# Attention's scores and values in 64x64 quarters of TensorE, and output stores into disjoint views, in an attention and two-MoE kernel

## The chip, the cores and the metric

The kernel runs on one core of one Trainium2 chip. The metric is the device time in microseconds (us) of one execution, as the median of several. Engines are named as the profile does: PE is TensorE, PEld its weight loads, DVE is VectorE, ACT is ScalarE, POOL is GpSimd, SP is SyncE.

## The reference, cut to what matters

Attention runs in chunks of 64 positions, each for itself, and two feed-forward stages follow.

```python
# q, k, v: [8 batches, 8 heads, 576 positions, 64]; chunks of 64 positions
scores = scale * np.matmul(q_c, k_c.transpose(0, 1, 2, 4, 3))
scores = scores - np.max(scores, axis=-1, keepdims=True)
attn = np.exp(scores)
attn = attn / (np.sum(attn, axis=-1, keepdims=True) + 1e-09)
out = np.matmul(attn, v_c)
...
x = out.transpose(0, 2, 1, 3).reshape(4608, 512)
h = x @ w_in
x = (h / (1.0 + np.exp(-h))) @ w_out
...
# each of the 4608 tokens goes to one of 8 experts, by x @ w_gate + bias
out[mask] = gate_w[mask, None] * (np.maximum(x[mask] @ w1[e], 0.0) @ w2[e])
```

Everything is f32. The large matmuls keep their precision by splitting each operand into a high part (type fp32r) and a low part, and by summing three products.

## The kernel before, in words

The 4608 tokens are 36 row tiles of 128 tokens, two chunks of 64 each, and 18 blocks of two tiles. For a tile, all 8 heads are handled at once; a head pair `hp` has the heads 2hp and 2hp+1.

The work has three stages. First, a list drawn up by a small planner (`order_of`, with costs and ranks written by hand) orders the attention of the tiles 0 to 5, the first layer of blocks 0 and 1, and the conversion of the first weights. Its scores (`early`, L478) and values (L521) already use 64x64 quarters of TensorE: 64 rows of the contraction by 64 output columns.

Second, for blocks j = 2 to 17, a loop of 18 steps a block does the first MoE layer of block j: `g1` (L615, 12 matmuls a step) and `g2` (L674 to L676). Between them stand pieces of the attention of the block after, at steps fixed in the lists `EVEN` and `ODD`, so that tile 6 and later tiles take this way. [...] For a tile the pieces are:

- `load_qk` (L357) and `load_nat` for v bring q and k in 32x32 pieces and v by rows, on SyncE's queue.
- `att_Tq` (L376) transposes q on VectorE in 32x32 pieces. `att_Tk` (L383) does so for k, a chunk at a time, and writes into `diag["k"]`, [128, 8 heads, 128], in which chunk c fills the rows and columns of half c; the rest stays zero. `diag_open` (L355) cleared it once on GpSimd.
- `att_S` (L395) has 8 matmuls, one a head: 128 contraction rows, 64 output partitions, 128 columns. The zeros keep the two chunks apart. All scores go to one bank of PSUM. Then follow maximum (L402), subtraction (L406) and exponential (L407).
- `att_norm` divides by the sum.
- `att_PT32` transposes p on TensorE (L434), and ScalarE copies it in two halves into `diag["p"]` (L437).
- `att_PV32` (L443) has 8 matmuls of the same shape, into one bank, and then `xh` (L451, ScalarE) and `xl` (L453, VectorE), the two parts of the MoE layer's input.

Scores, transposed p and values, and the ranks of the router (`place`, L773) share a pool of four banks (`ps_att`). The values of one tile and the scores of the next stand in the same step and so back to back on TensorE. VectorE also does the dot products of the router in these steps.

Third, the second MoE layer works through pairs of slots of 128 tokens each, with the expert's weights: `gather_id`, `gather` (L1086, rows by an indirect DMA on GpSimd's queue), `trans_x` (L1108, transposes the gathered rows on TensorE), `G1` (L1119), `G2` (L1145 to L1147). `finish(u)` scales the pair's two accumulators on ScalarE (L1226) and stores each by an indirect DMA (L1227), on GpSimd's queue too:

```python
for t, a in enumerate(oacc.pop(u)):
    ...
    nc.gpsimd.indirect_dma_start(out=out, out_offset=..., in_=o, ...)
```

Rows beyond a slot's count are dropped by the bounds check. The framework orders accesses to one DRAM tensor: a write to `out` waits until the write before it has landed. A slot for 32 tokens comes last (`lone_h`, `lone_T`, `lone_2`); its value matmuls (L1209) use four strips of 32 columns, and its output is stored at L1216.

Of the kernel before, what the change touches and what calls it, by code (L numbers as in the profile page):

```python
# [8 lines left out]

F32 = mybir.dt.float32  # L10
# [5 lines left out]
ALU = mybir.AluOpType  # L16
AX = mybir.AxisListType
# [3 lines left out]
P = 128  # L21
CH = 64
# [4 lines left out]
LQ = 4  # L27
# [177 lines left out]
def attention_moe_moe_kernel(  # L205
# [14 lines left out]
    nc = tc.nc  # L220
    B, H, S, D = q.shape
# [6 lines left out]
    HP = H // 2  # L228
# [35 lines left out]
    def ps_att():  # L264
        return ps.tile([P, 512], F32, tag="att", bufs=4, name="psa")

    def ps_h():
        return ps.tile([P, 512], F32, tag="h", bufs=2, name="psh")

    def ps_acc():  # L270
        return ps.tile([P, 512], F32, tag="acc", bufs=2, name="psc")

    def t2(name, dt=F32, shape=None):
        return sb.tile(shape or [P, 512], dt, tag="t2", bufs=11, name=name)
# [56 lines left out]
    nat, pairs = {}, {}  # L331
# [14 lines left out]

    late_p, diag = [], {}  # L350

    def diag_open():
        for n in ("k", "p"):
            diag[n] = late_p[0].tile([P, 8, P], F32, name="d" + n)
            nc.gpsimd.memset(diag[n], 0.0)  # L355

    def load_qk(t):  # L357
        x = t4("qk", shape=[P, 2, H, 2, 32])
# [12 lines left out]
    qkT = {}  # L371
# [6 lines left out]

    def att_Tk(t):
        x = nat.pop(("qk", t))  # L380
        for c in range(2):
            rows = slice(c * CH, (c + 1) * CH)
            nc.vector.transpose(  # L383
                diag["k"][rows, :, c * CH:(c + 1) * CH], x[rows, 1].rearrange("p h a d -> p h (a d)")
            )
            yield

    pexp = {}

    def att_S(t):  # L390
        sc = ps_att()
        qt = qkT.pop(("q", t))
        for h in range(H):
            hp, r = divmod(h, 2)
            nc.tensor.matmul(  # L395
                sc[r * CH:(r + 1) * CH, hp * P:(hp + 1) * P], lhsT=qt[:, h * CH:(h + 1) * CH],
                rhs=diag["k"][:, h, :], start=True, stop=True,
            )
        yield
        s3 = sc.rearrange("p (g c) -> p g c", c=CH)  # L400
        mx = sb.tile([P, 8, 1], F32, tag="mx", bufs=2, name="mx")
        nc.vector.tensor_reduce(out=mx, in_=s3, axis=AX.X, op=ALU.max)  # L402
        yield
        p = t2("p")
        p3 = p.rearrange("p (g c) -> p g c", c=CH)
        nc.vector.tensor_tensor(out=p3, in0=s3, in1=mx.to_broadcast([P, 8, CH]), op=ALU.subtract)  # L406
        nc.scalar.activation(out=p, in_=p, func=ACTF.Exp, scale=scale)  # L407
        pexp[t] = p

# [13 lines left out]
    def xT_of(t):  # L423
        j = t // 2
        if j not in xT:
            xT[j] = (t4("xh", F32R, [P, KD, 256]), t4("xl", F32R, [P, KD, 256]))
        return xT[j]

    def att_PT32(t):
        p = pexp.pop(t)  # L430
        pt = ps_att()
        for hp in range(HP):
            cols = slice(hp * P, (hp + 1) * P)
            nc.tensor.transpose(pt[:, cols], p[:, cols], ident)  # L434
        for c in range(2):
            rows = slice(c * CH, (c + 1) * CH)
            nc.scalar.copy(diag["p"][rows, :, c * CH:(c + 1) * CH], pt[rows].rearrange("p (h q) -> p h q", q=CH))  # L437

    def att_PV32(t):
        o, x = ps_att(), nat.pop(("v", t))  # L440
        for h in range(H):
            hp, r = divmod(h, 2)
            nc.tensor.matmul(  # L443
                o[r * CH:(r + 1) * CH, hp * P:(hp + 1) * P], lhsT=x[:, h, :], rhs=diag["p"][:, h, :],
                start=True, stop=True,
            )
        yield
        hi, lo = xT_of(t)
        cols = slice((t % 2) * P, (t % 2 + 1) * P)
        o3 = o.rearrange("p (k t) -> p k t", t=P)  # L450
        nc.scalar.copy(hi[:, :, cols], o3)  # L451
        yield
        nc.vector.tensor_tensor(out=lo[:, :, cols], in0=o3, in1=hi[:, :, cols].bitcast(F32), op=ALU.subtract)  # L453


    held = {}
# [84 lines left out]
    def load_w64(n):  # L541
        if n >= NF:
            return
        which, i = DS[n]
        if which == 0:
            a = conv.tile([P, KD, 2 * P, 2], U32, tag="raw", bufs=RAWB, name="ra")
            nc.sync.dma_start(out=a.rearrange("p k f w -> p k (f w)"), in_=w_in64[i])
        else:
            a = conv.tile([P, 2, 512, 2], U32, tag="raw", bufs=RAWB, name="rb")
            nc.sync.dma_start(out=a.rearrange("p a d w -> p a (d w)"), in_=w_out64[i])  # L550
        raw64[n] = a.rearrange("p a f w -> p (a f) w")
# [511 lines left out]
    oid = {}  # L1063
# [136 lines left out]
    def lone_2(ht):  # L1200

        a = ps_acc()
        n = DM // LQ
        for f in range(FE // P):
            g, i = divmod(f, FE // P // LQ)
            c = slice(i * P + g * LTOK, i * P + (g + 1) * LTOK)
            w = lone_w2[f]
            for m in range(LQ):
                nc.tensor.matmul(  # L1209
                    a[m * LTOK:(m + 1) * LTOK, :n], lhsT=ht[:, c], rhs=w[:, m * n:(m + 1) * n],  # L1210
                    start=f == 0, stop=f == FE // P - 1,
                )
        s = 2 * LONE
        o = t2("o")
        nc.scalar.activation(out=o[:, :n], in_=a[:, :n], func=ACTF.Copy, scale=idg[:, s, 1:2])
        nc.gpsimd.indirect_dma_start(  # L1216
            out=out.rearrange("n (h d) -> (n h) d", h=LQ),
            out_offset=bass.IndirectOffsetOnAxis(ap=oid["out"], axis=0), in_=o[:, :n], in_offset=None,
            bounds_check=LQ * NT - 1, oob_is_err=False,
        )  # L1220

    def finish(u):
        for t, a in enumerate(oacc.pop(u)):
            s = 2 * u + t
            o = t2("o")
            nc.scalar.activation(out=o, in_=a, func=ACTF.Copy, scale=idg[:, s, 1:2])  # L1226
            nc.gpsimd.indirect_dma_start(  # L1227
                out=out, out_offset=bass.IndirectOffsetOnAxis(ap=oid.pop(s), axis=0), in_=o, in_offset=None,
                bounds_check=NT - 1, oob_is_err=False,
            )  # L1230


    with tc.manual_schedule():
# [8 lines left out]
        def heat(n, pw=None):  # L1242

            pw = ps_h() if pw is None else pw
            for _ in range(n):
                nc.tensor.matmul(pw[:, :P], lhsT=ones, rhs=ones, start=True, stop=True)
# [55 lines left out]
        for n, idle in todo:  # L1302
            what = n[0]
            hps = None
            if what == "g1":
                st = n[2] + n[1] * SKEW
                begun = True
                if st not in gps:
                    gps[st] = ps_h()
                hps = gps[st][:, n[1] * 256:(n[1] + 1) * 256]  # L1310
            if idle > 0.3 and (hps is not None or not begun):
                heat(min(40, int(12 * idle)), hps)
            if what in ("qk", "v"):
                load_nat(n[1], what)
            elif what == "D":
                load_w64(n[1])
            elif what in RANK:
                early(*n)
            elif what == "g1":
                g1_mm(n[1], n[2], hps)  # L1320
            elif what == "g2":
                finish_step(n[1], n[2] + LAG)
            elif what in ("th", "g", "gh", "gl"):
                g_pair(*n)
            else:
                convert(*n)
            if n == ("lo", NF - 1):
                conv_cm.__exit__(None, None, None)
                late_cm = tc.tile_pool(name="late", bufs=1)
                late = late_cm.__enter__()  # L1330
                late_p.append(late)
                diag_open()
                wgb = late.tile([P, E, DM], F32, name="wgb")
                nc.sync.dma_start(
                    out=wgb.rearrange("p e d -> p (e d)"),
                    in_=wgt_d.rearrange("(o e) d -> o (e d)", o=1).to_broadcast([P, E * DM]),
                )
                wg.append(wgb)
            elif n == ("g2", 0, 1):
                router_loads()  # L1340
            elif n == ("g2", 0, 6):
                router_gate()
            elif n == ("g2", 0, NF - 4):
                zeros()
            elif n == ("g2", 1, NF - 3):
                router_bias()
            elif n == ("g1", 0, NF - 1):
                load_qk(2 * BLK32)
                load_nat(2 * BLK32, "v")
# [8 lines left out]
        for j in range(2, NB):  # L1358
            last = j == NB - 1
            side = {i: sides.pop(2 * nsteps * (j - 2) + i) for i in range(2 * nsteps)}  # L1360
            if last:
# [7 lines left out]
                for n in range(8):  # L1369
                    i, h = divmod(n, 2)  # L1370
# [99 lines left out]
        for u in range(STEADY):  # L1470
            for d in range(NS):
                if d < 2:
                    s = 2 * u + 2 + d
# [16 lines left out]
        u, d = behind.pop()  # L1490
# [67 lines left out]
```

## Time and profile before

| | |
|---|---|
| median of 3 runs | 1389.08 us (1388.49 to 1391.3) |
| the profiled execution | 1389.06 us |
| its span, first to last instruction | 1387.2 us |
| TensorE busy | 1360.8 us, 98% |
| weight loads | 1218.3 us, 88% |
| VectorE busy | 956.1 us, 69% |
| ScalarE busy | 597.7 us, 43% |
| GpSimd busy | 158.6 us, 11% |
| mean granted clock of TensorE | 0.994 |

Busy time is the time in which at least one instruction of an engine runs. Matmuls overlap in TensorE's pipeline, so an instruction's own duration is longer than its share of the time; the distance of two starts tells what one costs. In the rows below, `x16` counts records, and an f32 matmul leaves two of them, an fp32r matmul or a transpose one. Times in rows are us from the span's start; a mean or a minimum, median and maximum are ns; what stands behind `<-` in brackets is what ended the idle time ahead of an instruction.

### The profile page before, as it was taken

What the parts mean: (1) busy time and instruction counts of PE and PEld (TensorE: products, weight loads), DVE (VectorE), ACT (ScalarE), POOL (GpSimd) and SP (SyncE); (2) the same over time, 40 slices, a digit from 0 to 9 for tenths busy, and PEclk for the clock granted to TensorE, in tenths of its full rate; (3) what the DMA queues carried; (4) which work ended last, traced back from release to release, by engine and by line L of the source; (5) the groups of instructions that cost most, each with busy time, mean ns of one, the idle gap of its engine ahead of it and who ended that gap; (6) DMA issues with size and microseconds to landing.
All of it is one profiled execution on the core that took longest, in us unless ns stands there. A gap on an engine that the chain in (4) does not pass through costs nothing. (4 is left out here: it accounts for less than half of the span.)

```text
span 1387.2 us, 26517 instructions
## 1 busy us (share of the span) xinstructions
PE 1360.8 (98%) x9797; PEld 1218.3 (88%) x9797; DVE 956.1 (69%) x2358; ACT 597.7 (43%) x1220; POOL 158.6 (11%) x177
## 2 busy tenths in 40 slices
PE   8899999999999999999999999999999999999996
PEld 8788888988888888888898898888889889889985
DVE  5987886776777667677677677675577666666661
ACT  5554333333333333333333333342455555555551
POOL 1000000000000000000000000022322323232211
PEclk9899999999999999999999999999999999999999
DMA  9555521221231131132132120141676766667663
GB/s 213 170 166 168 108 50 27 50 55 35 34 61 33 32 62 35 28 62 47 16 62 50 27 48 24 37 117 32 233 261 217 233 214 225 215 222 226 227 194 125
DMA packets 242361, 153.93 MB, mean 111 GB/s; under 512 B 189408, under 2 KB 189446, under 8 KB 242096
## 3 DMA queue, kind: packets, MB, share of 16 engines
q1 hardware_dynamic: 234016, 133.07, 35.9%
q0 software_dynamic: 8208, 19.09, 3.8%
q8 instruction: 79, 1.29, 0.4%
q14 instruction: 58, 0.48, 0.1%
HBM read 132.48 MB, written 19.81 MB: 110 GB/s over the span
## 5 line engine op out<-in xcount | busy, mean ns | idle before, releaser
L615 PE MATMUL psh<-xh,big 128*128 128x256 f32 x2304 | 455.3, 283 | 0.0
L615 PEld LDWEIGHTS psh<-xh,big 128*128 128x128 f32 x2304 | 372.3, 189 | 12.4 <-issue 2.7
L615 PE MATMUL psh<-xl,big 128*128 128x256 f32 x1152 | 324.8, 282 | 0.1
L615 PEld LDWEIGHTS psh<-xl,big 128*128 128x128 f32 x1152 | 217.8, 189 | 9.2 <-DVE xl L532 0.3
L1119 PE MATMUL psh<-xgh,big 128*128 128x256 f32 x1152 | 216.4, 281 | 0.2 <-DVE big L922 0.2
L674 PE MATMUL psc<-big,g 128*128 128x512 f32 x512 | 206.4, 403 | 0.0
L624 DVE SCALAR_TENSOR_TENSOR g<-g,psh 128x256 f32<-128x256 f32 x256 | 107.3, 419 | 143.5 <-ACT g L623 139.9
L675 PE MATMUL psc<-big,g 128*128 128x512 f32 x512 | 202.8, 396 | 0.0
L676 PE MATMUL psc<-big,g 128*128 128x512 f32 x512 | 201.9, 394 | 0.7 <-DVE g L661 0.7
L696 DVE CUSTOM_DVE_ANT_0 dump<-x2t,wgb 128x512 bf16<-128x512 f32 x272 | 185.2, 681 | 8.3 <-ACT x2t L685 6.3
L623 ACT ACTIVATE g<-psh 128x256 f32<-128x256 f32 x256 | 98.0, 383 | 210.1 <-PE psh L615 199.0
L1119 PEld LDWEIGHTS psh<-xgh,big 128*128 128x128 f32 x1152 | 181.5, 188 | 3.7 <-DVE big L922 0.6
L659 ACT CAST g<-g 128x256 fp32r<-128x256 f32 x256 | 104.0, 406 | 153.5 <-DVE g L624 148.2
L1119 PE MATMUL psh<-xgl,big 128*128 128x256 f32 x576 | 161.8, 281 | 0.2 <-DVE xgl L1110 0.2
L1129 DVE SCALAR_TENSOR_TENSOR h<-psh,h 128x256 fp32r<-128x256 f32 x144 | 60.9, 424 | 128.6 <-ACT h L1128 118.1
L1128 ACT ACTIVATE h<-psh 128x256 fp32r<-128x256 f32 x144 | 55.4, 385 | 188.8 <-PE psh L1119 165.2
L793 POOL DMA_INDIRECT perm<-rpg,rdi x36 | 36.4, 1012 | 765.5 <-DVE rdi L792 639.0
L661 DVE TENSOR_TENSOR g<-g 128x256 fp32r<-128x256 f32 x256 | 107.7, 421 | 18.1 <-ACT g L659 18.1
L676 PEld LDWEIGHTS psc<-big,g 128*128 128x128 f32 x512 | 96.1, 188 | 24.4 <-DVE g L661 1.1
L1119 PEld LDWEIGHTS psh<-xgl,big 128*128 128x128 f32 x576 | 108.5, 188 | 3.5 <-DVE xgl L1110 0.5
L674 PEld LDWEIGHTS psc<-big,g 128*128 128x128 f32 x512 | 96.2, 188 | 15.4 <-ACT xh L451 2.4
L675 PEld LDWEIGHTS psc<-big,g 128*128 128x128 f32 x512 | 96.4, 188 | 12.5
(256 smaller groups left out, 2000.1 us busy)
## 6 DMA issues: line engine op xcount, KB each, us to landing
rb<-in_moe_w_dram SPq DMA_DIRECT2D x136, 256.0 KB
wr<-in_moe_w_dram SPq DMA_DIRECT2D x67, 512.0 KB
x2d<-x2t SPq DMA_DIRECT2D x36, 256.0 KB
ra<-in_moe_w_in_dram SPq DMA_DIRECT2D x8, 1024.0 KB
rb<-in_moe_w_out_dram SPq DMA_DIRECT2D x8, 1024.0 KB
qk<-in_q_dram SPq DMA_DIRECT2D x240, 32.0 KB
qk<-in_k_dram SPq DMA_DIRECT2D x240, 32.0 KB
vn<-in_v_dram SPq DMA_DIRECT2D x28, 256.0 KB
```

The source lines that it names most:

```text
L615: nc.tensor.matmul(hps[:, :256], lhsT=w, rhs=x[:, kk, :], start=n == 0, stop=n == 3 * KD - 1)
L623: nc.scalar.activation(out=g, in_=hps[:, :256], func=ACTF.Tanh, scale=0.5)
L624: nc.vector.scalar_tensor_tensor(out=g, in0=g, scalar=1.0, in1=hps[:, :256], op0=ALU.add, op1=ALU.mult)
L659: nc.scalar.copy(gh, g)
L661: nc.vector.tensor_tensor(out=gl, in0=g, in1=gh.bitcast(F32), op=ALU.subtract)
L674: nc.tensor.matmul(a, lhsT=gh[:, c], rhs=wh, start=f == 0, stop=False)
L675: nc.tensor.matmul(a, lhsT=gh[:, c], rhs=wl, start=False, stop=False)
L676: nc.tensor.matmul(a, lhsT=gl[:, c], rhs=wh, start=False, stop=f == NF - 1)
L696: nc.vector.tensor_tensor_reduce(out=dump, in0=x2[j][t], in1=wg[0][:, e, :], scale=1.0, scalar=0.0, op0=ALU.mult, op1=ALU.add, accum_out=l ...
L1119: nc.tensor.matmul(hp[:, :256], lhsT=w[:, part, :], rhs=x[:, :, kk * P:(kk + 1) * P], start=i == 0, stop=i == 3 * KD - 1,)
L1128: nc.scalar.activation(out=gh, in_=hp[:, :256], func=ACTF.Relu)
L1129: nc.vector.scalar_tensor_tensor(out=gl, in0=hp[:, :256], scalar=0.0, in1=gh.bitcast(F32), op0=ALU.max, op1=ALU.subtract)
```

## The change

Scores and values of tile 6 and later are computed without zero blocks. Each head and chunk has a matmul of its own, 64 contraction rows (the chunk's half c) by 64 output partitions (half r, the head's place in its pair) by 64 columns, so there are 16 of them instead of 8, in the order of `quarters()`: c = 0 with r = 0 and 1, then c = 1 with r = 0 and 1, for each head pair. Chunk 0 writes to one bank and chunk 1 to another, so scores take two banks and values two. k and p are transposed into plain tiles (`kT` and `pT`, two buffers each), by one instruction instead of two. Maximum, subtraction, `xh` and `xl` now have one instruction a bank. The zero blocks and their clearing are gone. The stores of the second MoE layer write into three views of `out` that the framework takes as disjoint: the pair's first tile, its second tile, and the last slot.

```diff
-    def diag_open():
-        for n in ("k", "p"):
-            diag[n] = late_p[0].tile([P, 8, P], F32, name="d" + n)
-            nc.gpsimd.memset(diag[n], 0.0)
+    def late_t(name):
+        return late_p[0].tile([P, 512], F32, tag=name, bufs=2, name=name)
...
     def att_Tk(t):
         x = nat.pop(("qk", t))
+        y = qkT["k", t] = late_t("kT")
+        nc.vector.transpose(y, x[:, 1].rearrange("p h a d -> p (h a d)"))
...
+    def quarters():
+
+        for hp in range(HP):
+            for c in range(2):
+                for r in range(2):
+                    yield hp, c, r, slice(c * CH, (c + 1) * CH), slice(r * CH, (r + 1) * CH)
+
+    def att_S(t):
+        sc = ps_att(), ps_att()
+        qt, kt = qkT.pop(("q", t)), qkT.pop(("k", t))
+        for hp, c, r, rows, out_rows in quarters():
+            h = slice((2 * hp + r) * CH, (2 * hp + r + 1) * CH)
+            nc.tensor.matmul(
+                sc[c][out_rows, hp * CH:(hp + 1) * CH], lhsT=qt[rows, h], rhs=kt[rows, h], start=True, stop=True
+            )
+        yield
+        s3 = [x[:, :HP * CH].rearrange("p (g k) -> p g k", k=CH) for x in sc]
+        mx = sb.tile([P, 8, 1], F32, tag="mx", bufs=2, name="mx")
         for c in range(2):
+            nc.vector.tensor_reduce(out=mx[:, c * HP:(c + 1) * HP], in_=s3[c], axis=AX.X, op=ALU.max)
+        yield
+        p = t2("p")
+        p4 = p.rearrange("p (g c k) -> p g c k", c=2, k=CH)
+        for c in range(2):
+            nc.vector.tensor_tensor(
+                out=p4[:, :, c, :], in0=s3[c], in1=mx[:, c * HP:(c + 1) * HP].to_broadcast([P, HP, CH]),
+                op=ALU.subtract,
             )
...
     def att_PT32(t):
...
-        for c in range(2):
-            rows = slice(c * CH, (c + 1) * CH)
-            nc.scalar.copy(diag["p"][rows, :, c * CH:(c + 1) * CH], pt[rows].rearrange("p (h q) -> p h q", q=CH))
+        pT[t] = late_t("pT")
+        nc.scalar.copy(pT[t], pt)
 
     def att_PV32(t):
-        o, x = ps_att(), nat.pop(("v", t))
-        for h in range(H):
-            hp, r = divmod(h, 2)
+        o, x, y = (ps_att(), ps_att()), nat.pop(("v", t)), pT.pop(t)
+        for hp, c, r, rows, out_rows in quarters():
+            h = 2 * hp + r
             nc.tensor.matmul(
-                o[r * CH:(r + 1) * CH, hp * P:(hp + 1) * P], lhsT=x[:, h, :], rhs=diag["p"][:, h, :],
+                o[c][out_rows, hp * CH:(hp + 1) * CH], lhsT=x[rows, h, :], rhs=y[rows, h * CH:(h + 1) * CH],
                 start=True, stop=True,
             )
...
+        for c in range(2):
+            nc.scalar.copy(hi[:, :, cols[c]], o3[c])
+        yield
+        for c in range(2):
+            nc.vector.tensor_tensor(
+                out=lo[:, :, cols[c]], in0=o3[c], in1=hi[:, :, cols[c]].bitcast(F32), op=ALU.subtract
+            )
...
-            out=out.rearrange("n (h d) -> (n h) d", h=LQ),
+            out=outs[2].rearrange("n (h d) -> (n h) d", h=LQ),
...
+    outs = dram_disjoint_views(out, 3)
...
-                out=out, out_offset=bass.IndirectOffsetOnAxis(ap=oid.pop(s), axis=0), in_=o, in_offset=None,
+                out=outs[t], out_offset=bass.IndirectOffsetOnAxis(ap=oid.pop(s), axis=0), in_=o, in_offset=None,
```

## Rows read from the trace of the kernel before

**Rows 1.** Busy: TensorE, weight loads, VectorE, ScalarE, GpSimd; granted clock; DMA share, GB/s
```profile
138.00:891.00 753.00, 752.99 (x5462) 673.04 (x5461) 541.58 (x1556) 275.99 (x645) 30.33 (x30) 1.00 0.23 44
891.00:1374.00 483.00, 478.33 (x3116) 430.23 (x3115) 305.65 (x648) 248.99 (x466) 119.37 (x114) 1.00 0.61 198
```

**Rows 2.** Groups by line: shapes, count, busy us, mean ns, idle before
```profile
L443 PE MATMUL psa<-dp,vn 128*64 128x128 f32 x480 | 32.8, 279 | 0.0
L395 PE MATMUL psa<-dk,qT 128*64 128x128 f32 x480 | 31.4, 273 | 0.0
```

**Rows 3.** TensorE in order of time: start, length, line, count
```profile
280.50 1.09 PE L443 MATMUL psa<-dp,vn 128*64 128x128 f32 x16
281.43 1.04 PE L395 MATMUL psa<-dk,qT 128*64 128x128 f32 x16
282.40 0.39 PE L615 MATMUL psh<-xh,big 128*128 128x256 f32 x1
```

**Rows 4.** TensorE in order of time, early tiles that use quarters
```profile
21.40 0.97 PE L521 MATMUL psa<-pT,nat 64*64 64x64 f32 x32
...
34.38 0.22 PE L478 MATMUL psa<-kT,qT 64*64 64x64 f32 x1
34.43 0.22 PE L521 MATMUL psa<-pT,vn 64*64 64x64 f32 x1
34.43 0.22 PE L478 MATMUL psa<-kT,qT 64*64 64x64 f32 x1
34.44 0.22 PE L521 MATMUL psa<-pT,vn 64*64 64x64 f32 x1
34.44 0.98 PE L478 MATMUL psa<-kT,qT 64*64 64x64 f32 x27
```

**Rows 5.** Busy time of L1209 alone in one stretch, four column strips
```profile
1374.49:1375.80 1.31, 1.31 (x48) 1.31 (x50) 1.00 0.00 0
```

**Rows 6.** Groups by line, VectorE: transpose, whole and half low parts
```profile
L383 DVE STREAM_TRANSPOSE dk<-qk 64x512 f32<-64x512 f32 x60 | 42.2, 703 | 0.9
L453 DVE TENSOR_TENSOR xl<-psa,xh 128x512 fp32r<-128x512 f32 x30 | 20.5, 682 | 2.0 <-ACT xh L451 2.0
L532 DVE TENSOR_TENSOR xl<-psa,xh 128x256 fp32r<-128x256 f32 x12 | 4.5, 416 | 0.6 <-ACT xh L530 0.6
```

**Rows 7.** Bank users, 279.5 to 313: ns min/median/max, first and last start
```profile
L443 PE MATMUL psa<-dp,vn x32: 272/273/324, 280.5 to 310.9; 128*64 128x128 f32 x32
L437 ACT COPY dp<-psa x2: 582/582/582, 301.7 to 302.3; 64x512 f32<-64x512 f32 x2
L773 PE MATMUL psa<-rob,triu x1: 180/180/180, 293.8 to 293.8; 128*128 128x8 bf16 x1
```

**Rows 8.** GpSimd at a pair's stores: queue waits, then order of time
```profile
L1227 POOLq EVENT_SEMAPHORE  x35: 17/2918/7207, 980.9 to 1374.7; - x35
...
996.04 1.28 POOL L1227 DMA_INDIRECT out_dram<-o,oi  x1 [10.40 <-ACT o L1226]
1003.47 1.01 POOL L1227 DMA_INDIRECT out_dram<-o,oi  x1 [6.14 <-DVE k_b L1012]
1004.78 1.06 POOL L1086 DMA_INDIRECT xrow<-x2d,oi  x1 [0.30 <-PE psa L1108]
```

**Rows 9.** TensorE's waits: for whom, us in total, times, longest
```profile
PE psa L1108 <- DMA xrow<-x2d,oi: 3.2, 5, 1.1
```

**Rows 10.** The end in order of time: GpSimd, ScalarE, last chain
```profile
1374.87 0.98 POOL L1227 DMA_INDIRECT out_dram<-o,oi  x1 [13.52 <-ACT o L1226]
1378.36 0.99 POOL L1227 DMA_INDIRECT out_dram<-o,oi  x1 [2.50 <-issue]
1382.27 0.98 POOL L1216 DMA_INDIRECT out_dram<-o,oo  x1 [2.93 <-DMA out_dram<-o,oi]
...
1376.82 0.37 ACT L1215 ACTIVATE o<-psc,idg 128x128 f32<-128x128 f32 x1 [1.53 <-PE psc L1209]
...
1378.36 3.15 DMA out_dram<-o,oi
```

More of the change, by code (lines that the diff above doesn't have):

```diff
@@ L7 @@
 from concourse._compat import with_exitstack
+from concourse.ap import dram_disjoint_views
 from concourse.masks import make_identity
@@ L345, in load_nat @@
                 nat[nm, t] = x
-    late_p, diag = [], {}
-    def diag_open():
-        for n in ("k", "p"):
-            diag[n] = late_p[0].tile([P, 8, P], F32, name="d" + n)
-            nc.gpsimd.memset(diag[n], 0.0)
+    late_p = []
+    def late_t(name):
+        return late_p[0].tile([P, 512], F32, tag=name, bufs=2, name=name)
     def load_qk(t):
@@ L380, in att_Tk @@
         x = nat.pop(("qk", t))
-        for c in range(2):
-            rows = slice(c * CH, (c + 1) * CH)
[L383 to L386, printed above, removed]
-    pexp = {}
+        y = qkT["k", t] = late_t("kT")
+        nc.vector.transpose(y, x[:, 1].rearrange("p h a d -> p (h a d)"))
+        return
+        yield
+    pexp = {}
+    def quarters():
[3 more added lines that the diff above has]
+                    yield hp, c, r, slice(c * CH, (c + 1) * CH), slice(r * CH, (r + 1) * CH)
     def att_S(t):
-        sc = ps_att()
-        qt = qkT.pop(("q", t))
-        for h in range(H):
-            hp, r = divmod(h, 2)
+        sc = ps_att(), ps_att()
+        qt, kt = qkT.pop(("q", t)), qkT.pop(("k", t))
+        for hp, c, r, rows, out_rows in quarters():
+            h = slice((2 * hp + r) * CH, (2 * hp + r + 1) * CH)
             nc.tensor.matmul(
-                sc[r * CH:(r + 1) * CH, hp * P:(hp + 1) * P], lhsT=qt[:, h * CH:(h + 1) * CH],
-                rhs=diag["k"][:, h, :], start=True, stop=True,
+                sc[c][out_rows, hp * CH:(hp + 1) * CH], lhsT=qt[rows, h], rhs=kt[rows, h], start=True, stop=True
             )
         yield
-        s3 = sc.rearrange("p (g c) -> p g c", c=CH)
+        s3 = [x[:, :HP * CH].rearrange("p (g k) -> p g k", k=CH) for x in sc]
         mx = sb.tile([P, 8, 1], F32, tag="mx", bufs=2, name="mx")
-        nc.vector.tensor_reduce(out=mx, in_=s3, axis=AX.X, op=ALU.max)
+        for c in range(2):
+            nc.vector.tensor_reduce(out=mx[:, c * HP:(c + 1) * HP], in_=s3[c], axis=AX.X, op=ALU.max)
         yield
         p = t2("p")
-        p3 = p.rearrange("p (g c) -> p g c", c=CH)
-        nc.vector.tensor_tensor(out=p3, in0=s3, in1=mx.to_broadcast([P, 8, CH]), op=ALU.subtract)
+        p4 = p.rearrange("p (g c k) -> p g c k", c=2, k=CH)
[4 more added lines that the diff above has]
+            )
         nc.scalar.activation(out=p, in_=p, func=ACTF.Exp, scale=scale)
@@ L427, in xT_of @@
         return xT[j]
+    pT = {}
     def att_PT32(t):
@@ L434, in att_PT32 @@
             nc.tensor.transpose(pt[:, cols], p[:, cols], ident)
-        for c in range(2):
-            rows = slice(c * CH, (c + 1) * CH)
-            nc.scalar.copy(diag["p"][rows, :, c * CH:(c + 1) * CH], pt[rows].rearrange("p (h q) -> p h q", q=CH))
+        pT[t] = late_t("pT")
+        nc.scalar.copy(pT[t], pt)
     def att_PV32(t):
-        o, x = ps_att(), nat.pop(("v", t))
-        for h in range(H):
-            hp, r = divmod(h, 2)
+        o, x, y = (ps_att(), ps_att()), nat.pop(("v", t)), pT.pop(t)
+        for hp, c, r, rows, out_rows in quarters():
+            h = 2 * hp + r
             nc.tensor.matmul(
-                o[r * CH:(r + 1) * CH, hp * P:(hp + 1) * P], lhsT=x[:, h, :], rhs=diag["p"][:, h, :],
+                o[c][out_rows, hp * CH:(hp + 1) * CH], lhsT=x[rows, h, :], rhs=y[rows, h * CH:(h + 1) * CH],
                 start=True, stop=True,
@@ L448, in att_PV32 @@
         hi, lo = xT_of(t)
-        cols = slice((t % 2) * P, (t % 2 + 1) * P)
-        o3 = o.rearrange("p (k t) -> p k t", t=P)
-        nc.scalar.copy(hi[:, :, cols], o3)
+        o3 = [z[:, :HP * CH].rearrange("p (k t) -> p k t", t=CH) for z in o]
+        cols = [slice((t % 2) * P + c * CH, (t % 2) * P + (c + 1) * CH) for c in range(2)]
+        for c in range(2):
+            nc.scalar.copy(hi[:, :, cols[c]], o3[c])
         yield
-        nc.vector.tensor_tensor(out=lo[:, :, cols], in0=o3, in1=hi[:, :, cols].bitcast(F32), op=ALU.subtract)
+        for c in range(2):
+            nc.vector.tensor_tensor(
+                out=lo[:, :, cols[c]], in0=o3[c], in1=hi[:, :, cols[c]].bitcast(F32), op=ALU.subtract
+            )
     held = {}
@@ L1331, in attention_moe_moe_kernel @@
                 late_p.append(late)
-                diag_open()
                 wgb = late.tile([P, E, DM], F32, name="wgb")
```

## The prediction

> **What bounds the kernel now.** I read the busy time by stretch first, then the groups by line, then the instructions in order of time around one block of scores, and last the waits and the output's stores. [...] The reader is to see two things in these rows: the first stretch is all TensorE, and the second has a few microseconds of holes.
>
> The matmuls that change are L395 (scores) and L443 (values): 480 records each, 31.4 and 32.8 us [rows 2]. Of 30 row tiles (6 to 35) each has 8 such matmuls per line and an f32 matmul leaves two records, so a block of 8 matmuls is 16 records, and there are 60 blocks.
>
> **TensorE, the main term.** In order of time, values start at 280.50, scores at 281.43, and the next layer's matmul at 282.40 [rows 3]. The scores' 16 records last 1.04 us; the last record alone is 0.27, so the starts spread over 0.77 us. Records start two at a time (two column halves work side by side), which makes 7 steps of 0.109 us; a block is 8 such steps, 0.872 us.
>
> A block now becomes 16 matmuls, 32 records, of half the rows and half the columns. The nearest rows are the early tiles, which already use quarters. There 27 score records spread over 0.98 - 0.22 = 0.76 us; two at a time, that is 13 steps of 0.0585 us [rows 4]. A record on 64 columns therefore takes 0.0585 us of its quarter. Those scores use only two of the quarters, the diagonal ones. But where the values' off-diagonal quarters overlap with them, the rows show four starts between 34.43 and 34.44, about 0.06 us after the starts at 34.38: all four quarters at once, at the same step [rows 4]. If that holds through a block, 32 records are 8 steps of 0.0585 = 0.468 us, and each block saves 0.404 us: 60 x 0.404 = 24.3 us. That is one end.
>
> The other end is how fast records can be sent at all. The fullest quarter stretch of the trace starts 32 records in 0.97 - 0.22 = 0.75 us, 24.2 ns each [rows 4]; with four column strips 48 records pass in 1.31 us, 27.3 ns each, and there the work itself sets the pace [rows 5]. Four quarters want 14.6 ns each, sustained, which no row shows for a whole block. At 24.2 ns a block is 0.774 us and the saving 60 x 0.098 = 5.9 us. I take the end of four at once, since it comes from the very same tiles and the same sizes, less 0.02 us a block for filling two more quarters: 23.1 us.
>
> The order of the new loop puts the two halves of columns of one row half next to each other. That these can run side by side is what L395 does today with its two column halves, and the strips of L1209 with four [rows 3, 5]. Two row halves write the same output partitions, into the two banks of `sc[c]` or `o[c]`.
>
> **VectorE and ScalarE, costed at nothing.** A tile's k loses one transpose of two (0.703 us). Maximum, subtraction and low part are each cut in two: the half-size operation takes 0.416 us (L532) against 0.682 for the whole (L453), so each pair adds 0.15 us, 0.45 together [rows 6]. Net, VectorE has 0.25 us less per tile. ScalarE writes pT in one copy instead of two of 0.582 us [rows 7]; `xh` becomes two. What covers all of these is TensorE's own work; should VectorE be late, its results (`g`, then the low part) would hold the second matmul, in at most the 0.25 us with the sign turned, 30 x 0.25 = 7.5 us. I take nothing. The two memsets of the old zero blocks ran on GpSimd ahead of all this, where nothing waited for them. The loads are the same transfers in the same order on SyncE's queue.
>
> **Banks, costed at nothing.** The pool of four banks now gives two to scores and two to values, and where values of one tile and scores of the next stand back to back they take all four. What held them last must then be read. Between two such places (values start at 280.5, and the last value record of the second place starts at 310.9) come only the ranks (293.8) and the transposes of p, which ScalarE has read by 302.3 + 0.6 = 302.9; the next four are wanted some 7 us later [rows 7]. So no wait. If a bank were still held, TensorE would stand with every later matmul behind it, and 0.1 us at each of some 28 such places would cost 2.8 us.
>
> **The stores.** Each pair of output tiles is stored by two indirect DMAs on GpSimd's queue. The wait ahead of the second lasts up to 7.2 us, median 2.9 over all waits at that line, and ends when the first has landed: 996.04 and 1003.47 are 7.4 us apart, though one takes only 1 us of the engine [rows 8]. The gather of the next slot's rows stands behind it in the queue, at 1004.78. TensorE waited five times for such rows, 3.2 us in all, up to 1.1 [rows 9]. With views the second store needs only the previous pair's second, which landed long ago, and the gather goes some 5 us earlier. Bounds are 0 (the gather then waits for its own buffer) and 3.2 us, plus some for waits put down to other things; I take 2.6, since 1.1 us earlier is enough for each. No store of the same view can overtake a wait: GpSimd still works its queue in order.
>
> At the end three stores are in a row at 1374.87, 1378.36 and 1382.27; the second's transfer ends at 1378.36 + 3.15 = 1381.51, and only then does the third go [rows 10]. Its input is ready at 1376.82 + 0.37 = 1377.19. Stores pitched at 1.3 us, as the store and gather at 1003.47 and 1004.78 are [rows 8], put the third at 1377.5: 4.8 us earlier. Three transfers in flight may land a little later, so I take 4.4; the bounds are 0 and 4.8.
>
> **Sum.** The profiled execution took 1389.06 us (span 1387.2), the median of the runs is 1389.08, so one stands for the other. 1389.06 - 23.1 - 2.6 - 4.4 = 1359.0 us.
>
> **Rivals.**
> *Sending limits.* Records pass at 24.2 ns instead of 14.6, and everything else is as above: 1389.06 - 5.9 - 7.0 = 1376.2; anything between the two rates lies between 1359 and 1376. For it: no row shows a faster rate over a block. Against: in the row of 32 records two quarters' own steps account for the pace. [...] I give it 0.16.
>
> *Two at a time.* If records must start in program order, the second half of a matmul waits for the first in its own quarter and only overlaps with the next matmul's first: two per step, 16 steps of 0.0585 = 0.936 us, 0.064 more than now. 1389.06 + 3.8 - 7.0 = 1385.9. Against it are the strips, in which four records go per 0.109 us although each matmul's two are neighbours [rows 5]. [...] 0.07.
>
> *Slower: weights that cannot be loaded beside a neighbour.* Two of each four matmuls share a row half. If a load had to wait until that half is silent, a half would do its 16 records one by one, with a load at least as long as the pass between: 16 x 0.117 = 1.87 us a block, 1.0 us more: 1389.06 + 60 - 7 = 1442. The point at which it decides is whether the second matmul of a row half starts with the first or after it. Against it: L395 loads and runs two column halves of one row range in step [rows 3]. [...] 0.05.
>
> *The cover goes.* TensorE's stretch is full only just; VectorE has 72% of it. If half the saved time came back as waits for `g`, 1389.06 - 11.6 - 7.0 = 1370.5. 0.06.
>
> *The views free nothing*, because the stores wait for something else than each other: 1389.06 - 23.1 = 1366. The waits' ends at landings speak against it. 0.04.
>
> **Chances and range.** The forecast has 0.62. About 0.2% (2.8 us) is what a measurement can tell from no change. Faster: 0.62 + 0.16 + 0.06 + 0.04, and 0.03 of two at a time, which lies on the edge: 0.91. Same: the other 0.04. Slower: 0.05. All gains at their upper bounds give 1389.06 - 24.3 - 3.2 - 4.8 = 1356.8, so the range starts at 1355 for the waits not put down to the stores. Up to 1375 it holds the forecast, the last two rivals and half of the sending limit: 0.80.
>
> **What would show it.** Right: 32 records per block, spread over some 0.5 us; scores and values back to back taking about 1.1 us instead of 1.90; TensorE still busy throughout the attention stretch; the second store some 1.3 us behind the first; no wait for gathered rows; the three last stores within 3 us. Wrong: a block that lasts 0.75 us or more, new waits of TensorE for banks or for VectorE, or a second store that still waits for a landing.

## The result and the profile after

The changed kernel takes 1356.57 us (median of 4 runs, 1355.19 to 1356.9) against 1389.35 us before in the same set of runs, a ratio of 0.976 with a 95% interval of 0.9743 to 0.9777. The profiled execution took 1356.82 us, its span 1355.1 us, 32.1 us less than before; the spans are compared below. Line numbers of the changed kernel are mostly 3 to 15 higher.

The busy time by stretch, with the columns of [rows 1]; the first stretch ends here with the last values, where in [rows 1] it ends 5 us behind them:

```profile
138.00:862.00 724.00, 724.00 (x6381) 647.69 (x6383) 520.12 (x1601) 257.62 (x639) 30.15 (x30) 1.00 0.24 46
862.00:1346.40 484.40, 482.77 (x3173) 435.09 (x3163) 308.47 (x664) 251.34 (x472) 123.04 (x114) 1.00 0.61 198
```

TensorE is busy 724.00 of the 724.00 us of the first stretch, as free of holes as in [rows 1], so what it saved there came off the end in full. In the second it now lacks 1.6 us instead of 4.7. The instructions in order of time around one place where values and scores adjoin, as in [rows 3]:

```profile
276.11 0.69 PE L451 MATMUL psa<-pT,vn 64*64 64x64 f32 x32
276.62 0.65 PE L398 MATMUL psa<-kT,qT 64*64 64x64 f32 x32
277.20 0.39 PE L627 MATMUL psh<-xh,big 128*128 128x256 f32 x1
```

Values, scores and the step to the next layer's matmul take 1.09 us instead of 1.90, 0.81 less for two blocks. The 32 score records end 0.65 us after the first start, the last one lasting 0.22: 0.43 us of starts, where 7 steps of 0.0585 and three starts of 7 ns make 0.43. So four records start in every step: here the first four at 276.621, 276.628, 276.635 and 276.641, the next one at 276.680.

How long the attention lasts is read from the instructions of the two lines (count, duration in ns as min/median/max, first and last start), from the first score record to the last value record; this "attention stretch" serves in the experiments too:

```profile
L398 PE MATMUL psa<-kT,qT x960: 218/218/267, 148.2 to 842.5; 64*64 64x64 f32 x192
L451 PE MATMUL psa<-pT,vn x960: 218/218/268, 164.9 to 862.1; 64*64 64x64 f32 x192
```

That is 862.1 - 148.2 = 713.9 us. Before, it was 885.8 - 148.1 = 737.7 us, so the difference is 23.8 us:

```profile
L395 PE MATMUL psa<-dk,qT x480: 272/273/323, 148.1 to 865.8; 128*64 128x128 f32 x160
L443 PE MATMUL psa<-dp,vn x480: 272/273/324, 165.3 to 885.8; 128*64 128x128 f32 x160
```

For the orders tried below, the first block of scores serves too. It follows other work, and its first step takes 0.107 us instead of 0.0585, so its starts spread over 0.69 - 0.22 = 0.48 us (in order of time, the last record lasting 0.22):

```profile
148.19 0.69 PE L398 MATMUL psa<-kT,qT 64*64 64x64 f32 x32
```

VectorE and ScalarE in the groups by line (columns as in [rows 6]):

```profile
L405 DVE TENSOR_REDUCE mx<-psa 128x4 f32<-128x256 f32 x60 | 22.6, 419 | 11.7 <-PE psa L398 11.7
L463 DVE TENSOR_TENSOR xl<-psa,xh 128x256 fp32r<-128x256 f32 x60 | 22.4, 414 | 0.8 <-ACT xh L460 0.8
L380 DVE STREAM_TRANSPOSE kT<-qk 128x512 f32<-128x512 f32 x30 | 21.1, 704 | 0.0
L445 ACT COPY pT<-psa 128x512 f32<-128x512 f32 x30 | 17.6, 587 | 6.9 <-PE psa L443 6.9
```

The half-size operations take 0.414 and 0.419 us, the transpose of 128 partitions as long as that of 64 did (0.704 and 0.703). VectorE waits for scores 11.7 us in all where it had waited 33.6.

GpSimd's queue at a pair's stores, its waits at that line and then the order of time, as in [rows 8]:

```profile
L1242 POOLq EVENT_SEMAPHORE  x34: 17/42/8526, 951.1 to 1346.7; - x34
...
996.52 1.28 POOL L1242 DMA_INDIRECT out_dram<-o,oi  x1 [5.52 <-ACT o L1241]
998.11 1.00 POOL L1242 DMA_INDIRECT out_dram<-o,oi  x1 [0.30 <-ACT h L1140]
999.41 1.04 POOL L1098 DMA_INDIRECT xrow<-x2d,oi  x1 [0.30 <-issue]
```

The second store goes 1.6 us after the first instead of 7.4, and the median wait is 42 ns instead of 2918. TensorE has no wait for gathered rows any more [rows 9], and the end looks so [rows 10]:

```profile
1346.90 0.98 POOL L1242 DMA_INDIRECT out_dram<-o,oi  x1 [19.70 <-ACT o L1241]
1348.19 0.99 POOL L1242 DMA_INDIRECT out_dram<-o,oi  x1 [0.30 <-issue]
1349.48 0.98 POOL L1228 DMA_INDIRECT out_dram<-o,oo  x1 [0.30 <-issue]
```

Laid side by side by the starts of TensorE's matmuls, the 32.1 us of the span are: attention stretch 23.8 less; from there to the first matmul of the second MoE layer 0.6 more; that layer up to the last slot 4.8 less; its value matmuls 0.3 and the stores behind them 3.8 less.

### The profile page after: what moved, and what is told of

Read it like the earlier page. It is cut to its first block, busy times and chain, and to the rows that moved or that the text cites. A ratio compares the mean times of both kernels' runs of the same rounds, so it can differ in the third digit from the quotient of the medians.

```text
span 1355.1 us, 28404 instructions
## 1 busy us (share of the span) xinstructions
PE 1335.6 (99%) x10757; PEld 1197.3 (88%) x10757; DVE 937.4 (69%) x2418; ACT 580.9 (43%) x1220; POOL 160.2 (12%) x175
## 4 chain that ended last, share of the span: by engine, by line
PE 91%; DVE 3%; issue 3%; DMA 2%; ACT 1%; SPq 1%; POOL 0%; POOLq 0%; ACTq 0%; DVEq 0%
PE psh L627 30%; PE psh L1131 14%; PE psc L686 10%; PE psc L687 9%; PE psc L688 9%; PE psc L1157 2%; PE psc L1158 2%; PE psc L1159 2%; PE psa L1158 2%; PE psa L1157 2%; PE psa L1159 2%; PE psa L451 1%; PE psa L398 1%; PE psa L1120 1%; PE psa L443 1%
## 5 line engine op out<-in xcount | busy, mean ns | idle before, releaser
L1131 PE MATMUL psh<-xgh,big 128*128 128x256 f32 x1152 | 216.5, 281 | 0.2 <-DVE big L934 0.2
L688 PE MATMUL psc<-big,g 128*128 128x512 f32 x512 | 202.2, 395 | 1.3 <-DVE g L673 1.3
L1131 PEld LDWEIGHTS psh<-xgh,big 128*128 128x128 f32 x1152 | 181.4, 188 | 3.7 <-DVE big L934 0.6
L1131 PE MATMUL psh<-xgl,big 128*128 128x256 f32 x576 | 161.7, 281 | 0.2 <-DVE xgl L1122 0.2
L688 PEld LDWEIGHTS psc<-big,g 128*128 128x128 f32 x512 | 96.3, 188 | 25.0 <-DVE g L673 1.9
L1131 PEld LDWEIGHTS psh<-xgl,big 128*128 128x128 f32 x576 | 108.5, 188 | 3.5 <-DVE xgl L1122 0.5
```

The lines of the kernel that those rows point to most:

```text
L688: nc.tensor.matmul(a, lhsT=gl[:, c], rhs=wh, start=False, stop=f == NF - 1)
L1131: nc.tensor.matmul(hp[:, :256], lhsT=w[:, part, :], rhs=x[:, :, kk * P:(kk + 1) * P], start=i == 0, stop=i == 3 * KD - 1,)
```

## The experiments

Every run is told with its time and, where it matters, the attention stretch from the same profile. Three sets of runs were made, each on one chip: first the four runs down to one quarter after another; then scores twice, the old copies, a pair in one view and the early order; last two head pairs a quarter and the three repeats under the stall. A single time without a range is one run. Diffs are against the changed kernel, except the second.

**The stores undone.**

```diff
-    outs = dram_disjoint_views(out, 3)
+    outs = (out, out, out)
```

> The changed kernel with its stores into out itself again, as before. Theory (the two parts of the change add up): the attention stretch keeps its 23.8 us, the waits for gathered rows (4.6 us by starts) and the landing ahead of each of the last stores (4.1 us) come back: 1356.6 + 8.7 = 1365.3 us. Rival (the quarters alone carry it, and the stores' waits were hidden): 1357 to 1359 us.

1364.39 us (1363.63 to 1365.61), ratio to before 0.9821 (0.9804 to 0.9837). The attention stretch is 862.7 - 148.8 = 713.9 us, as in the changed kernel. What the transposes of gathered rows wait for on TensorE (us in total, times, longest), and the last stores in order of time:

```profile
PE psa L1120 <- DMA xrow<-x2d,oi: 1.7, 2, 1.5
```
```profile
1349.68 0.98 POOL L1242 DMA_INDIRECT out_dram<-o,oi  x1 [15.01 <-ACT o L1241]
1355.47 0.98 POOL L1242 DMA_INDIRECT out_dram<-o,oi  x1 [4.81 <-issue]
1358.93 0.98 POOL L1228 DMA_INDIRECT out_dram<-o,oo  x1 [2.47 <-DMA out_dram<-o,oi]
```

The sum is near what was expected, its parts are not: two waits for rows return, not six (2.1 us from start to start instead of 4.6), and the end costs more, since the first of the last stores took 5.8 us until the second could go.

**The stores alone**, in the kernel before: `outs` and its uses as in the change, attention untouched.

> The kernel before with the three views alone, attention with its zero blocks. Theory: 1389.3 - 4.6 - 4.1 = 1380.6 us, no gap of TensorE ahead of the transposes of gathered rows, last three stores 1.3 us apart. Rival (gathers then wait for their own buffers, so only the end is shorter): 1385.2 us. Rival (stores wait for something else than each other): 1389 us.

1380.95 us (1379.91 to 1382.73), ratio 0.9945 (0.9929 to 0.9962). The transposes of gathered rows have no idle time ahead of them (groups by line), and the last stores stand 1.3 us apart (order of time):

```profile
L1109 PE MATMUL psa<-ident,xrow 128*128 128x128 f32 x144 | 21.6, 272 | 0.0
```
```profile
1370.76 0.98 POOL L1230 DMA_INDIRECT out_dram<-o,oi  x1 [19.69 <-ACT o L1229]
1372.05 0.99 POOL L1230 DMA_INDIRECT out_dram<-o,oi  x1 [0.31 <-issue]
1373.34 0.98 POOL L1217 DMA_INDIRECT out_dram<-o,oo  x1 [0.30 <-issue]
```

Against the 1389.57 us of before in this set, the views alone give 8.6 us and the quarters alone 25.2. Their sum, 33.8, is within the spread of the runs what both give together (32.8). The parts add up.

**Another order of the quarters.**

```diff
-        for hp in range(HP):
-            for c in range(2):
-                for r in range(2):
+        for off in range(2):
+            for hp in range(HP):
+                for c in range(2):
+                    r = c ^ off
```

> The changed kernel with the order of the quarters as the early tiles have it: all 8 matmuls of the diagonal quarters, then all 8 of the others; everything else equal. Theory (TensorE starts records of different quarters out of program order, but looks only some 6 unstarted matmul records ahead, as the early values show): 5 to 6 steps with two quarters at either end, 13 steps of 0.0585 us a block instead of 8, 0.29 us more; 60 x 0.29 = 17.5 us, less up to 4.9 us where scores begin under values: 1369 to 1374 us. Rival (it looks ahead freely): 1356.6 us. Rival (two at a time whenever the order pairs them): 16 steps, 28 us more, 1385 us.

The early values are these rows of before, in order of time: six records of one tile (`nat`) start at 24.58 or later, after the next tile's first (`vn`) at 24.54.

```profile
24.54 0.27 PE L521 MATMUL psa<-pT,vn 64*64 64x64 f32 x1
24.58 0.28 PE L521 MATMUL psa<-pT,nat 64*64 64x64 f32 x3
24.64 0.22 PE L521 MATMUL psa<-pT,vn 64*64 64x64 f32 x1
24.64 0.28 PE L521 MATMUL psa<-pT,nat 64*64 64x64 f32 x3
```

1368.48 us. The first scores in order of time, and the two lines with their first and last starts:

```profile
148.10 0.97 PE L399 MATMUL psa<-kT,qT 64*64 64x64 f32 x32
```
```profile
L399 PE MATMUL psa<-kT,qT x960: 218/218/267, 148.1 to 854.2; 64*64 64x64 f32 x192
L452 PE MATMUL psa<-pT,vn x960: 218/218/268, 165.1 to 874.0; 64*64 64x64 f32 x192
```

The stretch is 725.9 us, 12.0 longer, just under the 12.6 to 17.5 that were expected. This block's starts spread over 0.75 us instead of 0.48: with the same 32 records in the same quarters and banks, the order alone costs this.

**One quarter after another.**

```diff
-        for hp in range(HP):
-            for c in range(2):
-                for r in range(2):
+        for c in range(2):
+            for r in range(2):
+                for hp in range(HP):
```

> The changed kernel with all four head pairs of one quarter first, then the next quarter. Theory (a look ahead of some 6 unstarted records): the second quarter starts 2 steps after the first, the third at step 6, the fourth at step 9, so a block is 17 steps of 0.0585 us, 0.99 us instead of 0.47, 0.53 us more; 60 x 0.53 = 31.6 us, less up to 8 us where scores begin under values: 1380 to 1388 us. Rival (free look ahead): 1356.6 us. Rival (strict program order): 32 steps, 84 us more, 1440 us.

1402.09 us, slower than before the change. The same two views:

```profile
148.27 1.54 PE L398 MATMUL psa<-kT,qT 64*64 64x64 f32 x32
```
```profile
L398 PE MATMUL psa<-kT,qT x960: 218/218/268, 148.3 to 887.4; 64*64 64x64 f32 x192
L451 PE MATMUL psa<-pT,vn x960: 218/218/268, 165.9 to 907.8; 64*64 64x64 f32 x192
```

The stretch is 759.5 us, 45.6 longer, or 0.76 us a block where 0.53 was expected: no rival fits, and the theory falls short. This block's starts spread over 1.32 us instead of 0.48. The trace doesn't name the quarters, but the first record of each lasts 0.267 us and the later ones 0.218. In these records the first quarter's starts come alone at 148.271, 148.377, 148.436 and 148.494, and the second quarter's first only with the fifth, at 148.552 and 148.558: three of the first quarter's eight were then unstarted. Where values and scores adjoin it is the same, in order of time: the first score starts at 167.00, ahead of three value records.

```profile
165.85 1.36 PE L451 MATMUL psa<-pT,vn 64*64 64x64 f32 x29
167.00 0.27 PE L398 MATMUL psa<-kT,qT 64*64 64x64 f32 x1
167.06 0.22 PE L451 MATMUL psa<-pT,vn 64*64 64x64 f32 x1
167.11 0.22 PE L398 MATMUL psa<-kT,qT 64*64 64x64 f32 x1
167.11 0.22 PE L451 MATMUL psa<-pT,vn 64*64 64x64 f32 x1
167.17 0.22 PE L398 MATMUL psa<-kT,qT 64*64 64x64 f32 x1
167.17 0.22 PE L451 MATMUL psa<-pT,vn 64*64 64x64 f32 x1
```

In the order with the diagonals first, six were unstarted (the first two scores there start from 165.71 on, six value records at 165.76 to 165.88), but three in each of two quarters. So it looks as if what stops the rest is one quarter that holds about three waiting records, an estimate from these starts alone, and a count over all quarters the wrong picture.

**Two head pairs a quarter**, to tell these two pictures apart:

```diff
-        for hp in range(HP):
+        for half in range(2):
             for c in range(2):
                 for r in range(2):
-                    yield hp, c, r, slice(c * CH, (c + 1) * CH), slice(r * CH, (r + 1) * CH)
+                    for hp in (2 * half, 2 * half + 1):
+                        yield hp, c, r, slice(c * CH, (c + 1) * CH), slice(r * CH, (r + 1) * CH)
```

> The changed kernel with the order of the quarters changed once more: each quarter gets two head pairs (four records) in a row before the next quarter. Theory, as the two orders above have left it (records go out in program order, each quarter holds some 3 that wait, and only a full quarter stops the rest): a quarter's four records are taken in as soon as its first has started, so a block stays at 8 or 9 steps, and the attention stretch within 0 to 3.5 us of the changed kernel's 714.06. Rival (6 unstarted records in all): the fourth quarter starts about 2 steps late, and the stretch is about 7 us longer.

Of its TensorE, the first scores in order of time (start, time to the last end), then the two lines with their first and last starts:

```profile
148.32 0.76 PE L399 MATMUL psa<-kT,qT 64*64 64x64 f32 x32
```
```profile
L399 PE MATMUL psa<-kT,qT x960: 218/218/267, 148.3 to 846.4; 64*64 64x64 f32 x192
L452 PE MATMUL psa<-pT,vn x960: 218/218/268, 165.1 to 866.0; 64*64 64x64 f32 x192
```

The stretch is 717.7 us, 3.8 longer: 0.063 us a block, one step. That is a hair above what the picture of three waiting records a quarter gave, and half of what six in all would have cost. The first starts show it more plainly: 148.320, 148.333, 148.346 and 148.360, each of 0.267 us and so, by that sign, in four different quarters. When the fourth went, nine records ahead of it in the program had not started, three in each of three quarters. (The run's time, 1367.16 us, holds the stall of the third set, below.)

**Scores twice.**

```diff
-        for hp, c, r, rows, out_rows in quarters():
+        for hp, c, r, rows, out_rows in [*quarters(), *quarters()]:
```

> The changed kernel with the 16 score matmuls of each tile issued twice over (the second writes the same values again). Theory (a block is 8 steps of four records and nothing more once TensorE is in quarters): 30 x 0.468 = 14.0 us more, 1370.6 us. Rival (a block has its own fixed cost, such as the 0.32 us between the last matmul before it and its first record): 30 x 0.7 = 21 us more, 1377.6 us.

Of its TensorE, the first scores in order of time (start, time to the last end), then the two lines with their first and last starts:

```profile
148.60 1.16 PE L398 MATMUL psa<-kT,qT 64*64 64x64 f32 x64
```
```profile
L398 PE MATMUL psa<-kT,qT x1920: 218/218/267, 148.6 to 857.0; 64*64 64x64 f32 x192
L451 PE MATMUL psa<-pT,vn x960: 218/218/268, 165.8 to 876.5; 64*64 64x64 f32 x192
```

1378.91 us seems to speak for the rival, but the stretch is 727.9 us, 14.0 longer, as the theory had it: 0.467 us for 32 more records, 14.6 ns each. Of the other 8.3 us 7.5 are lost in the second MoE layer, which this edit does not touch (see the stall, below).

**The old number of transposes and copies.**

```diff
-        nc.vector.transpose(y, x[:, 1].rearrange("p h a d -> p (h a d)"))
+        for c in range(2):
+            rows = slice(c * CH, (c + 1) * CH)
+            nc.vector.transpose(y[rows], x[rows, 1].rearrange("p h a d -> p (h a d)"))
+            yield
...
-        nc.scalar.copy(pT[t], pt)
+        for c in range(2):
+            rows = slice(c * CH, (c + 1) * CH)
+            nc.scalar.copy(pT[t][rows], pt[rows])
```

> The changed kernel with k transposed by two instructions on VectorE (0.703 us more a tile) and p copied by two on ScalarE (0.576 us more a tile), as before the change; TensorE's work as in the changed kernel. Theory (both engines are covered by TensorE): 1356.6 us, within 1.5 us. Rival (part of the gain comes from the work taken off them): up to 30 x 0.7 = 21 us more, 1378 us.

1363.80 us (1363.1 to 1364.92), 7 us over what was expected, but not where VectorE or ScalarE work for the attention: the stretch is 863.1 - 148.2 = 714.9 us, 1.0 longer, though both engines do as much there as before, by the groups of lines:

```profile
L382 DVE STREAM_TRANSPOSE kT<-qk 64x512 f32<-64x512 f32 x60 | 42.2, 703 | 0.9
L448 ACT COPY pT<-psa 64x512 f32<-64x512 f32 x60 | 34.9, 582 | 7.5 <-PE psa L444 7.0
```

**A pair in one view.**

```diff
-                out=outs[t], out_offset=bass.IndirectOffsetOnAxis(ap=oid.pop(s), axis=0), in_=o, in_offset=None,
+                out=outs[0], out_offset=bass.IndirectOffsetOnAxis(ap=oid.pop(s), axis=0), in_=o, in_offset=None,
```

> The changed kernel with both stores of a pair in one view and only the last slot's store in a view of its own. Theory: the second store waits for the first's landing again, so the waits for gathered rows return (4.6 us), and at the end the second of the last stores goes 2.2 us later and the third right behind it: 1356.6 + 4.6 + 2.2 = 1363.4 us. Rival (the end alone matters): 1358.8 us.

The last stores on GpSimd's queue, in order of time:

```profile
1349.40 0.98 POOL L1242 DMA_INDIRECT out_dram<-o,oi  x1 [14.90 <-ACT o L1241]
1352.90 0.99 POOL L1242 DMA_INDIRECT out_dram<-o,oi  x1 [2.51 <-issue]
1354.19 0.98 POOL L1228 DMA_INDIRECT out_dram<-o,oo  x1 [0.30 <-issue]
```

1362.08 us (1361.56 to 1362.62). The end is as expected, with the third store 4.8 us after the first instead of 2.6: though its view is its own, it goes 1.3 us behind the second, so GpSimd's queue kept its order. Of the 4.6 us of waits for rows only one of 1.5 us returns (1.7 from start to start); another 1.4 us belong to the stall of this set.

**The early tiles in the rotating order**, a try to better the changed kernel:

```diff
-            for hp, a, r in [(hp, a, a) for hp in range(HP) for a in range(2)] + [
-                (hp, 1 - r, r) for hp in range(HP) for r in range(2)
-            ]:
+            for hp, a, r in [(hp, a, r) for hp in range(HP) for a in range(2) for r in range(2)]:
```

> The changed kernel with the early tiles' value matmuls (tiles 0 to 5) in the rotating order too, their banks and everything else as they are. Theory: their blocks shrink from 0.75 to 0.47 us, 6 x 0.28 = 1.7 us at most; TensorE waits for other engines in that stretch, so 0 to 1.7 us less: 1354.9 to 1356.6 us. Rival (the list of the early stage shifts its waits or TensorE's clock): slower by up to a few us.

1363.12 us (1362.51 to 1363.43), while the first score record of tile 6 starts at 148.1 as ever: nothing gained, nothing lost in the early stage. Again the second MoE layer is longer.

**The stall.** All four kernels of the second set lost time in the same place of the second MoE layer, three of them with the edit elsewhere: 5.1 to 7.5 us by the starts of the layer's matmuls, and 1.4 in the run with a pair in one view. So the changed kernel itself ran again beside two of them.

> The changed kernel itself, beside the two kernels that stood still for 3 to 5 us in the second MoE layer while ScalarE, VectorE and SyncE issued slowly. Theory (that stall belongs to the chip and place of a run, not to the edits): it shows the same stall here, 1360 to 1364 us. Rival (it belongs to the edits): 1356.6 us and no such stall.

1362.74 us (1360.71 to 1363.02), ratio to the 1387.79 us of before in this set 0.982 (0.9804 to 0.9837). SyncE's queue in order of time, here and, in the second fence, in the first profile of the same kernel:

```profile
948.09 0.40 SPq L922 DMA_DIRECT2D wr<-in_moe_w_dram  x1
950.59 2.15 SPq L929 DMA_DIRECT2D rb<-in_moe_w_dram  x2
953.45 0.00 SPq L922 DMA_DIRECT2D wr<-in_moe_w_dram  x1
954.89 2.13 SPq L929 DMA_DIRECT2D rb<-in_moe_w_dram  x2
```
```profile
948.59 0.40 SPq L922 DMA_DIRECT2D wr<-in_moe_w_dram  x1
949.26 0.95 SPq L929 DMA_DIRECT2D rb<-in_moe_w_dram  x2
950.42 0.39 SPq L922 DMA_DIRECT2D wr<-in_moe_w_dram  x1
951.07 0.93 SPq L929 DMA_DIRECT2D rb<-in_moe_w_dram  x2
```

What takes 3.4 us in one takes 8.9 in the other, and in the longer one idle time of ScalarE and VectorE is put down to no other engine (waits for whom, us in total, times, longest):

```profile
ACT h L1140 <- issue: 5.6, 1, 5.6
DVE h L1141 <- issue: 4.8, 1, 4.8
ACT h L1140 <- remote: 3.3, 1, 3.3
```

TensorE is busy 7.18 of 10 us behind them, and in the 4 us after that its mean granted clock is 0.57 instead of 1.00 (columns as in [rows 1]):

```profile
950.00:960.00 10.00, 7.18 (x41) 5.61 (x40) 1.18 (x3) 1.08 (x3) 4.96 (x5) 1.00 0.97 336
960.00:964.00 4.00, 4.00 (x16) 3.43 (x16) 2.01 (x3) 1.92 (x3) 0.00 (x0) 0.57 0.64 234
```

The same matmuls (L1157 to L1159) start 0.427 us apart from 960 to 964 us and 0.235 at 1.00, and from the transposes ahead of them (L1120) to the next L1131 it takes 4.64 us instead of 3.24 in the first profile. So at least 1.4 of the 5.7 us that the layer loses up to the last slot (by starts) are the clock's. In the run with a pair in one view TensorE stayed busy for 9.04 of the same 10 us and the clock at 1.00; in the two that lost most, 7.1 and 7.5 us, the mean clock of the profiled run was 0.991 and 0.992, against 0.995 with a pair in one view.

> The kernel with the second transpose and the second copy once more, beside the changed kernel. Theory (both engines are covered, the 7 us over were that stall): within 1.5 us of the changed kernel of the same call, attention stretch 715 us. Rival: 7 us slower than it.

1362.71 us (1362.17 to 1364.12), stretch 862.9 - 147.9 = 715.0.

> The kernel with the rotating order in the early tiles once more, beside the changed kernel. Theory (the early stage waits for other engines, so the order there gives nothing, and the 6.5 us over were that stall): within 1.5 us of the changed kernel of the same call. Rival (the early order itself costs): 6 us slower than it.

1361.66 us (1360.22 to 1363.52). Both are as fast as the changed kernel of their set, within the spread of its runs. The stall goes with the set, not with the edits: the old copies cost at most 1 us, and the early order nothing that can be told.

## Why the prediction was right

The forecast was 1359.0 us, and the time is 1356.57, in the range and with the mechanism named as likeliest. It lies a hair below the sum with all gains at their upper bounds, 1356.8. What keeps it in the range is the margin for waits not put down to the stores, and that is what came: 2.0 of the 2.4 us are gathered rows.

- **The matmuls.** 23.1 us were forecast and 23.8 came. The end of four at once, 24.3, was nearer than the 0.02 us a block taken off it; filling two more quarters costs three starts of 7 ns once, not in each step. The forecast rests on a burst of four starts; that it holds through a block was a bet, and it came out. That an order of the quarters must feed all four was shown by turning it: the diagonals first cost 12 us, quarter after quarter 45.6.
- **The rivals there.** Sending is no limit: 32 records more cost 14.6 ns each in the run with the scores twice, what four quarters want. Between different quarters starts are 7 ns apart. Nor do records start in strict program order: in the run with one quarter after another, the second quarter's first record starts at 148.558 and the first quarter's sixth at 148.611. Two in one row half also ran side by side, four starts in every step of 0.0585 us, so the slower rival fell at its deciding point.
- **VectorE and ScalarE at nothing.** Their old work put back changes the stretch by 1.0 us. The cover slips once: at 891 us, in the last block's steps, TensorE waits 1.3 us for the low part of `g`, where it waited 0.7 before. That is the 0.6 us lost behind the attention stretch.
- **Banks at nothing.** TensorE had no wait for one; in the whole stretch from 138 to 862 us it was busy without a gap. No wait hides in the distance of starts either: it is the same to 0.01 us at all places of a kind (0.32 us from L688 to values, 0.15 from scores to the next layer's matmul).
- **The gathered rows** were mis-sized: 2.6 us forecast under a bound of 3.2, and 4.6 came. The bound was read from idle time, five waits in [rows 9]. Counted from start to start of TensorE's matmuls there were six gaps, of 1.27, 0.98, 0.93, 0.59, 0.42 and 0.40 us beyond the usual step; the longest counts as 1.11 us of idle time. An engine whose last matmul is still running out counts as busy although nothing new starts.
- **The end.** 4.4 forecast, 4.1 came: 3.8 behind the last matmuls and 0.3 in a gap among them, which was not looked for.

What the prediction lacked altogether is the stall: the variants of the second set and the changed kernel itself in the third lose some 6 us more (the pair in one view less), and the gain over before shrinks to 25.1 us (ratio 0.982). What starts it is open; a part of its price is TensorE's clock (at least 1.4 of 5.7 us, at a mean of 0.57). Before has no profile from those chips, so whether it stalls there and elsewhere makes up for it wasn't seen.

## What to carry to other kernels

Where the contraction and the output are 64 each, as here, quarters were worth most in an order that visits another quarter with every matmul; the starts of the same 16 matmuls spread over 0.48, 0.54, 0.75 or 1.32 us by their order alone. Of the 23.8 us that the attention gained, two matmuls a quarter lost 3.8 and the diagonals first 12.0, and quarter after quarter made it slower than with the zero blocks. The two row halves, which write the same partitions, had a bank each here; whether one bank would do wasn't tried. Stores that never overlap should be told so to the framework when something urgent stands behind them in the same queue, and what a wait costs TensorE is better read from the distance of starts than from its idle time (4.6 us against 3.2 here).

## What the runs showed of the hardware that was not expected

- TensorE's records started out of program order across quarters: with one quarter after another, the first score at 167.00 and three value records ahead of it in the program at 167.06 to 167.17. That a quarter takes in about three that wait, and that the next record for a full quarter stops all behind it, is an estimate from the starts in the runs with other orders; it fits those with 8, 4 and 2 records in a row (1.32, 0.54 and 0.48 us of starts), and the diagonals (0.75).
- Four records of four quarters start 7 ns apart, every 58.5 ns, through all 60 blocks of the changed kernel's profile (but for a first step of 0.107 us behind other work), and scores follow values without a gap.
- In two of the sets SyncE, ScalarE and VectorE issued slowly at once for some 9 us in the second MoE layer, at the same place of the program in each profile (in the changed kernel's, SyncE took 8.9 us for what took 3.4, and ScalarE and VectorE stood up to 5.6 and 4.8 us). In the changed kernel's profile there TensorE, busy 7.18 of 10 us behind them, then ran for 4 us at a mean granted clock of 0.57. Why they issue slowly is not shown.
